# A new order and new engines for the tasks between two phases of an attention and mixture-of-experts kernel

## The chip, the cores and the metric

The kernel runs on one core of a Trainium2 chip. A core has five engines that run side by side, each with its own queue of instructions in a fixed order: TensorE (PE: matrix products and transposes), VectorE (DVE), ScalarE (ACT), GpSimd (POOL, which here also issues the indirect transfers) and SyncE (SP, which issues the other transfers). They wait for one another through semaphores. The metric is the time of one execution in microseconds (us); lower is better. It was measured three times before the change, and once more under the profiler.

## What is computed

Linear attention, and behind it a layer of eight experts in which each token goes to one:

```python
# q, k, v: 8 batches x 8 heads x 576 tokens x 64
q_s = softmax(q, axis=-1);  k_s = softmax(k, axis=2)        # k over the tokens
kv  = einsum('bhsd,bhse->bhde', k_s, v)
x   = einsum('bhsd,bhde->bhse', q_s, kv)  ->  (8, 576, 512)
logits = x @ w_gate                        # 8 experts
gate   = sigmoid(x @ w_local)
for b, s in order:
    e = argmax(logits[b, s]) if s == 0 or gate[b, s] < 0.5 else the expert of token s-1
    out[b, s] = softmax(logits[b, s])[e] * (relu(x[b, s] @ w1[e]) @ w2[e])
```

w1 is 512 x 1024 and w2 1024 x 512 for each expert. There are 4608 tokens.

## The kernel before, in words

**Stages.** For each of the eight batches b a k/v pair is loaded and reduced to one product per head: tasks `Lk, Lv, max, kT, kr, ka, sub, exp` (the exponential of k), `vc` (v copied beside a column of ones), `mul` (the product, PE), `nsum, norm` (divided by its sums), `turn, hi, lo, KW, put` (its product with the gate's weights). "The first product of the seventh pair" is `mul.6.0`. The q side runs over four tiles t of two batches and nine pieces c of 128 x 512: `Lq` loads, `qm` takes the maxima, `qs` subtracts them (line 431), `qT` turns the piece on PE (line 440), `qe` takes the exponential (ACT, line 443), `xm` multiplies with the k/v products into PSUM (line 455), `xc` copies the result to SBUF (line 190 on ACT, 192 on DVE), and after three pieces `inv, xs, ex, gs` take the reciprocals, store the rows to DRAM (888 KB) and form the gate's logits.

**Choosing.** When tiles 0 and 1 are through, `g, Sa, Sb, g1 to g4, ra, rp, rb, ac` (mostly DVE) find each token's expert and its rank, `ro.t.c` (18 of them for these tiles; line 614 on DVE, two instructions of lines 618 and 619 on ACT) write one-hot rows, `ab, am, ax` turn them into the row indices `gidx` (line 678), and `ai, aj` say which expert each block has. `Sc` and the store `Sd.0` give each token's share.

**Blocks.** Tokens are sorted by expert into blocks of 128. The first nine, the early blocks, hold tokens of tiles 0 and 1 alone, so they start while tiles 2 and 3 are still under way. `W.0` to `W.3` load the first expert's weights in quarters of 1 MB (SP). Each weight is cut into a high and a low half-precision part, in 16 pieces: `Wh.i` (line 190) and `Wl.i` (line 955 on DVE; on POOL two instructions), `Wh.12` to `Wh.15` from `W.3`. `G.b` gathers a block's rows (POOL, line 844), `Gp.b` its shares, `Px, Ph, Pl` scale and cut them, and `T.0` (PE) or the transfer `D.b` (SP, line 880) turns them. `F1.b.g` and `F2.b.g` (lines 903, 906 and 926) are the halves of the block's two products, `Ar, Al` the activation in two parts between them, `Gv, Pt` the scaled output and its store. `RN` and `s1, s2` renew the weights where the next block has another expert.

**What sets the order.** All of these tasks are registered with an engine, and some with a second one. A list written out by hand, `ORDER`, gives the order in which they are emitted, and so each engine's queue; the names in `SWAP` go to their second engine. Buffers are rings that are handed round in the order of emission: three for `qs`, three for the copied rows `xt`, two PSUM buffers `pq` shared by `qT`, `turn`, `KW`, `g1`, `rp` and `am`, and for tiles 2 and 3 one, `px`, between `xm` and `xc`. The engine and the registration of the tasks named here:

```python
        eng = alt if name in self.swap else eng                                    # line 65
        add(("Wh", i), ACT, cut_hi, alt=DVE, after=[("W", i // 4)])                # line 1092
        add(("Wl", i), DVE, cut_lo, alt=POOL, after=[("Wh", i)])
```

Of the kernel before, what the change touches and what calls it, by code (L numbers as in the profile page):

```python
# [104 lines left out]


SWAP = """
Ph.0 Ph.11 Ph.2 Ph.3 Ph.4 Ph.6 Ph.9 Pl.6 Pl.8 Px.0 Px.10 Px.4 Px.5 Px.6 Px.9 Wh.15 ex.1.2 ex.3.0 ex.3.2 gs.0.0 gs.0.1 gs.0.2 gs.1.0 gs.1.1
gs.2.0 gs.2.1 gs.2.2 gs.3.0 gs.3.2 norm.3 norm.5 norm.6 put.0 put.2 put.3 put.4 put.6 put.7 qs.2.4 qs.3.6 qs.3.7 ro.0.0 ro.0.2 ro.0.3 ro.0.5 ro.0.7
ro.0.8 ro.1.3 ro.1.7 ro.2.0 ro.2.1 ro.2.2 ro.2.4 ro.2.6 ro.3.0 ro.3.4 ro.3.6 sub.6.1 vc.0.0 vc.0.1 vc.1.0 vc.2.0 vc.3.0 vc.4.0 vc.4.1 vc.5.0 xc.0.0  # L110
xc.0.2 xc.3.5 xc.3.8
"""
# [19 lines left out]
nsum.7 ro.0.0 xm.2.4 ro.0.1 ro.0.4 norm.7 ow ro.0.6 ai turn.6 xc.2.4 hi.6 Lq.3.1 W.0 lo.6 qe.2.6 ro.1.2 xm.2.5 xc.2.5 turn.7 aj.p0 hi.7 lo.7 ex.2.0
ro.1.7 qT.2.7 qe.2.7 qs.2.8 qT.2.8 qe.2.8 ro.1.6 gs.2.0 KW.6 ro.1.5 ro.0.2 xm.2.6 xc.2.6 qs.3.0 qs.3.1 put.6 qT.3.0 xm.2.7 ro.0.5 xc.2.7 ro.0.7 qs.3.2
KW.7 put.7 qe.3.0 xm.2.8 xc.2.8 ab.p0 ro.0.8 qT.3.1 qe.3.1 W.1 inv.2.1 ex.2.1 xs.2.1 qs.3.3 Wh.6 qs.3.4 Wh.3 xm.3.0 xc.3.0 ro.1.0 ab.p1 aj ab ro.1.8
Wh.7 Wh.0 qm.3.1 am ax.p0 ax Wl.3 qT.3.2 qe.3.2 xm.3.1 xc.3.1 qT.3.3 qe.3.3 Wh.1 Sc.0 Wl.7 Wl.0 qT.3.4 Wl.6 qs.3.5 qs.3.6 qs.3.7 G.0 G.1 xm.3.2 xc.3.2
Px.0 Ph.0 Pl.0 qT.3.5 qe.3.5 W.2 qe.3.4 Sd.0 xm.3.3 xc.3.3 qT.3.6 Wh.2 xm.3.4 xc.3.4 Wl.1 W.3 G.2 G.3 Wh.5 Wh.4 qT.3.7 Wl.2 T.0 Tc.0 G.4 Wh.11 Wh.12
Px.1 inv.2.2 xm.3.5 xc.3.5 Wl.4 F1.0.0 Wh.10 Wl.5 qs.3.8 Wh.9 qe.3.6 xs.2.2 qT.3.8 Wl.10 Wl.9 Gp.0 Ph.1 Pl.1 ex.2.2 qe.3.7 xm.3.6 Wh.8
Wl.11 Wl.8 D.1 s1.0 Ar.0.0 Al.0.0 RN.1.0 xc.3.6 F1.0.1 Wl.12 qe.3.8 Wh.13 xm.3.7 Wh.15 Wl.15 Gp.1 Gp.2 xc.3.7 Ar.0.1 F2.0.0 Gp.3 F1.1.0
Al.0.1 RN.1.1 s1.1 Wl.13 Wh.14 gs.2.2 Wl.14 xm.3.8 xc.3.8 Px.2 G.5 G.6 s2.0 Ph.2 Pl.2 Ar.1.0 F2.0.1 RN.1.2 Al.1.0 Gv.0 RN.1.3 gs.2.1
F1.1.1 RN.2.1 Px.3 D.2 RN.2.0 inv.3.1 Px.4 ex.3.1 Ph.3 Pt.0 F2.1.0 Ph.4 Ar.1.1 Pl.3 D.3 Al.1.1 G.7 F1.2.0 Px.5 Ar.2.0  # L140
Al.2.0 s2.1 RN.2.2 Pl.4 D.4 s1.2 RN.3.0 inv.3.2 inv.3.0 gs.3.1 ex.3.2 Ph.5 F2.1.1 Gv.1 F1.2.1 F2.2.0 RN.2.3 ex.3.0 gs.3.0 s2.2 RN.3.2
Ar.2.1 Al.2.1 F1.3.0 RN.3.1 s1.3 F2.2.1 RN.4.0 gs.3.2 g.1.p0 G.8 Px.6 Ph.6 Ar.3.0 Pt.1 oh Gv.2 g.1.p1 g.1 Al.3.0 Pt.2 F1.3.1 g1.1
RN.4.1 F2.3.0 g2.1 g3.1 Ar.3.1 F1.4.0 Al.3.1 g4.1 ra.1 rp.1 Pl.5 RN.3.3 bc.p0 bc.p1 Pl.6 s2.3 D.5 bc D.6 bi.p0 Ar.4.0 Al.4.0
F2.3.1 Gv.3 bi Px.7 Ph.7 Px.8 RN.4.2 Pt.3 RN.4.3 F1.4.1 F2.4.0 rb.1.p0 s1.4 RN.5.0 Ar.4.1 xs.3.0 rb.1 ro.2.8 ro.3.7 RN.5.1 F1.5.0 Gp.4
ro.2.4 ro.2.6 s2.4 RN.5.2 Al.4.1 bb.p0 Pl.7 D.7 F2.4.1 Ar.5.0 Al.5.0 ro.2.5 F1.5.1 Ph.8 Pl.8 bj.p0 s1.5 bj.p1 xs.3.1 bj.p2 RN.6.0 Gv.4
Pt.4 ro.3.0 bj.p3 bj.p4 Ar.5.1 RN.5.3 RN.6.1 Gp.5 Al.5.1 Gp.6 bj ro.2.3 s1.6 F2.5.0 ro.3.8 Gp.7 xs.3.2 F1.6.0 bb bo.2 bo.1
ro.3.4 Ar.6.0 Al.6.0 ro.3.3 F2.5.1 ro.3.5 Sa.1 ro.2.0 Gv.5 RN.7.0 s2.5 RN.6.2 F1.6.1 Ar.6.1 ro.2.2 RN.7.1 RN.6.3 F2.6.0 F1.7.0 bo.3 D.8
Al.6.1 ro.3.6 s2.6 F2.6.1 ro.3.1 s1.7 RN.8.0 ro.2.1 Gv.6 Ar.7.0 RN.7.3 RN.7.2 bo.0 ro.3.2 bm.3 ro.2.7 Al.7.0 bm.1 bm.2 bm.0 bx.p0 bx
Sb.1 F1.7.1 Pt.5 Ar.7.1 Sc.1 Al.7.1 F2.7.0 F1.8.0 F2.7.1 s2.7 G.9 RN.8.2 Px.9 Ph.9 G.10 G.11 Pt.6 RN.8.1 s1.8 RN.8.3 s2.8
Px.10 Pl.9 Ar.8.0 Al.8.0 RN.9.0 Gv.7 Px.11 Ph.10 Pl.10 F1.8.1 T.9 RN.9.1 Tc.9 Sd.1 s1.9.0 s1.9.1 G.12 Ar.8.1 Al.8.1 F2.8.0 T.10 Tc.10 Pt.7 Ph.11 Pl.11  # L150
Gp.8 Gp.9
"""


# [1099 lines left out]
```

## Time and profile before

| | |
|---|---|
| three runs | 545.34, 548.05, 548.52 us (median 548.05) |
| the profiled execution | 545.22 us, of which the span 543.4 us |
| busy over the span | PE 494.1 us (91%), DVE 278.2 (51%), POOL 253.6 (47%), ACT 220.8 (41%) |
| one weight quarter / one store of rows | 1024.0 KB / 888.0 KB |

The page cuts the span into 40 slices of 13.6 us; PE's busy tenths there:

```profile
PE   1668796787999999999999999999999999999995
```

Up to the tenth slice PE has gaps, from the eleventh on it is full to the end. A busy PE is not yet a fast one: its clock is granted at one of two levels (1.2 and 2.4 GHz), and the profile gives it in each stretch as a share of the full one.

### The profile page before, as it was taken

Reading aid. Unit: us, or ns where it says so; the run is one execution under the profiler, and the core shown is the slowest. Engines: PE = TensorE matmul, PEld = TensorE weight load, DVE = VectorE, ACT = ScalarE, POOL = GpSimd, SP = SyncE. Lnnn points to the kernel's source line nnn. Section 1 sums busy time; section 2 is a strip of 40 time slices with the busy share of each in tenths; the row PEclk is TensorE's granted clock in tenths of the full one; section 3 lists DMA queues with packets and bytes.
Section 4 is the critical chain, followed back from the end, with each engine's and each line's share of the span. In section 5 each row is a group of like instructions: output and inputs, shape, how many; then the busy total and the mean of one; then the engine's idle time right before and its main releaser. Section 6 shows DMA issues by size and latency. Waiting matters only on the chain. (4 is left out here: it accounts for less than half of the span.)

```text
span 543.4 us, 19390 instructions
## 1 busy us (share of the span) xinstructions
PE 494.1 (91%) x7314; PEld 367.2 (68%) x7314; DVE 278.2 (51%) x505; ACT 220.8 (41%) x388; POOL 253.6 (47%) x280
## 2 busy tenths in 40 slices
PE   1668796787999999999999999999999999999995
...
GB/s 310 374 382 310 279 331 391 158 336 197 135 82 83 126 112 298 213 244 231 83 83 275 196 75 147 272 130 89 159 295 117 75 73 85 86 84 70 100 76 63
DMA packets 83822, 98.17 MB, mean 181 GB/s; under 512 B 44895, under 2 KB 61279, under 8 KB 83680
## 3 DMA queue, kind: packets, MB, share of 16 engines
...
## 5 line engine op out<-in xcount | busy, mean ns | idle before, releaser
L903 PE MATMUL ph<-xT,w1h 128*128 128x128 f16 (+1 forms) x2432 | 179.9, 217 | 0.4 <-issue 0.4
L903 PEld LDWEIGHTS <-w1h 128*128 128x128 f16 x2432 | 144.3, 98 | 1.3 <-issue 1.3
L933 POOL DMA_INDIRECT out<-y,sidx x38 | 40.0, 1053 | 177.5 <-ACTq L971 150.4
L915 DVE SCALAR_TENSOR_TENSOR lo<-ph,hi 128x512 f16<-128x512 f32 x76 | 52.3, 689 | 133.3 <-ACTq L971 126.5
L911 ACT ACTIVATE hi<-ph 128x512 f16<-128x512 f32 x76 | 45.3, 596 | 176.0 <-PE ph L903 122.8
L906 PE MATMUL ph<-xT,w1l 128*128 128x128 f16 (+1 forms) x1216 | 115.4, 217 | 0.9 <-issue 0.9
L906 PEld LDWEIGHTS <-w1l 128*128 128x128 f16 x1216 | 81.7, 98 | 17.6 <-issue 0.7
L926 PEld LDWEIGHTS <-hi 128*128 128x128 f16 x608 | 56.0, 98 | 54.4
L926 PE MATMUL py<-w2h,hi 128*128 128x512 f16 x184 | 69.8, 379 | 0.0
L926 PE MATMUL py<-w2h,lo 128*128 128x512 f16 x184 | 69.7, 379 | 0.0
L926 PE MATMUL py<-w2l,hi 128*128 128x512 f16 x184 | 69.7, 379 | 0.0
L867 DVE SCALAR_TENSOR_TENSOR x<-xn,x 128x512 f16<-128x512 f32 x39 | 31.7, 812 | 71.5 <-ACT x L190 70.6
L844 POOL DMA_INDIRECT xg<-xrows,gidx x42 | 48.9, 1163 | 23.8 <-DVE tz L679 12.1
L926 PEld LDWEIGHTS <-lo 128*128 128x128 f16 x304 | 29.7, 98 | 35.9
L926 PE MATMUL pi<-w2h,hi 128*128 128x512 f16 x120 | 45.5, 379 | 0.0
L926 PE MATMUL pi<-w2l,hi 128*128 128x512 f16 x120 | 45.5, 379 | 0.0
L926 PE MATMUL pi<-w2h,lo 128*128 128x512 f16 x120 | 45.5, 379 | 0.0
L850 POOL DMA_INDIRECT pb<-shares,gidx x39 | 41.3, 1060 | 8.2 <-issue 7.2
L431 POOL TENSOR_TENSOR qs<-qt,qm 128x512 f32<-128x512 f32 x33 | 34.8, 1065 | 19.0 <-PE pq L440 17.5
L855 POOL TENSOR_TENSOR xn<-xg 128x512 f32<-128x512 f32 x35 | 37.1, 1062 | 9.0 <-DVEq L971 3.2
L322 DVE TENSOR_REDUCE KM<-KT 128x128 f32<-128x1152 f32 x16 | 34.5, 2167 | 4.9 <-DMA KT<-in_k 4.9
L455 PE MATMUL px<-R,qe 64*64 64x74 f32 x864 | 24.5, 256 | 13.2 <-ACT xt L190 6.1
...
## 6 DMA issues: line engine op xcount, KB each, us to landing
...
xrows<-xt SPq DMA_DIRECT2D x12, 888.0 KB
...
s<-in_moe_w SPq DMA_DIRECT2D x4, 1024.0 KB
```

The source lines that it names most:

```text
L322: nc.vector.tensor_reduce(out=KM[b % 2][:, 2 * u:2 * u + 2], in_=KT[b % NKT][:, u:KG:2].rearrange("p g c d -> p g d c"), axis=AX.X, op=ALU ...
L431: on("qs", t, c).tensor_tensor(out=qs[t, c].rearrange("p (g x) d -> p g x d", x=2), in0=qt[t, u][:, :, i, :].rearrange("p (x g) d -> p g x ...
L844: nc.gpsimd.indirect_dma_start(out=xg[b % AHEAD], out_offset=None, in_=src, in_offset=bass.IndirectOffsetOnAxis(ap=i_[:, j_:j_ + 1], axis=0))
L850: nc.gpsimd.indirect_dma_start(out=pb[b % NPB], out_offset=None, in_=src, in_offset=bass.IndirectOffsetOnAxis(ap=i_[:, j_:j_ + 1], axis=0))
L855: eng.tensor_tensor(out=xn[b % 2].rearrange("p (g x d) -> p g x d", g=4, x=2), in0=xg[b % AHEAD].rearrange("p (g x) -> p g x", g=4)[:, :, ...
L867: nc.vector.scalar_tensor_tensor(out=x2[b % 2][:, 1, :], in0=xn[b % 2], scalar=XS, in1=x2[b % 2][:, 0, :], op0=ALU.mult, op1=ALU.subtract)
L903: nc.tensor.matmul(ph_[:, f, 0:n], W["w1h"][:, c, fs], xT_[:, i, c, 0:n], start=False, stop=(c == 3 and i == 1))
L906: nc.tensor.matmul(ph_[:, f, 0:n], W["w1l"][:, c, fs], xT_[:, 0, c, 0:n], start=(c == 0), stop=False)
L911: nc.scalar.activation(hi[b % 2][:, 4 * g:4 * g + 4, :], phs[g], AF.Relu)
L915: nc.vector.scalar_tensor_tensor(out=lo[b % 2][:, gs_, :], in0=phs[g], scalar=0.0, in1=hi[b % 2][:, gs_, :], op0=ALU.max, op1=ALU.subtract)
L926: nc.tensor.matmul(result(b), h_[:, f, :], w_[:, f, :], start=(f == 0 and i == 0), stop=(f == 7 and i == 2))
L933: nc.gpsimd.indirect_dma_start(out=outr, out_offset=bass.IndirectOffsetOnAxis(ap=i_[:, j_:j_ + 1], axis=0), in_=ys[b % 2], in_offset=None, ...
```

## The change

The list `ORDER` is rewritten from behind `mul.6.0` to the middle of the early block 1, and `SWAP` with it; all in front and all behind is as before (the first 321 of 799 names and the last 231 keep their places, the 247 between them are put in another order). Thirty-one tasks change their engine. From POOL to DVE go `qs.2.6, 2.7, 2.8, 3.0, 3.2, 3.3, 3.5, 3.8`, `gs.2.0` to `gs.2.2`, `ex.2.2, ex.3.1, Px.1, Px.2`; from ACT to DVE `norm.6, put.6, put.7, ro.0.0, ro.0.7, ro.1.7`; from DVE to ACT `ro.0.1, ro.1.0, ro.1.2, ro.1.4, ro.1.8, xc.3.5, Wh.15`; from ACT to POOL `vc.7.0, vc.7.1`; from DVE to POOL `Wl.2`. No task is added or removed.

```diff
 SWAP = """
-Ph.0 Ph.11 Ph.2 Ph.3 Ph.4 Ph.6 Ph.9 Pl.6 Pl.8 Px.0 Px.10 Px.4 Px.5 Px.6 Px.9 Wh.15 ex.1.2 ex.3.0 ex.3.2 gs.0.0 ...
+vc.0.0 vc.0.1 put.0 vc.1.0 vc.2.0 put.2 vc.3.0 norm.3 put.3 vc.4.0 vc.4.1 put.4 vc.5.0 norm.5 sub.6.1 vc.7.0 vc.7.1 ...
 ORDER = """
...
-xc.1.8 inv.1.2 exp.7.0 ex.1.1 gs.1.1 put.4 ex.1.2 gs.1.2 exp.6.0 qT.2.1 qe.2.1 xm.2.0 xc.2.0 qT.2.2 qe.2.2 qs.2.3 qT.2.3 mul.6.0 vc.6.1 qe.2.3 ...
+xc.1.8 inv.1.2 exp.7.0 ex.1.1 gs.1.1 put.4 ex.1.2 gs.1.2 exp.6.0 qT.2.1 qe.2.1 xm.2.0 xc.2.0 qT.2.2 qe.2.2 qs.2.3 qT.2.3 mul.6.0 exp.7.1 xs.1.2 ...
...
```

On ACT, from the copies of tile 3 to block 0's activation. `COPY xt` is `xc`, `qe` is `qe`, `w1h` and `w2h` are the cuts `Wh`, `x` is `Ph.1` and `hi` is `Ar.0.0`. Before:

```order
L190 ACTIVATE w1h<-s_1934 128x4x128
L190 COPY xt<-px 128x592
L190 ACTIVATE w1h<-s_1934 128x4x128 x2
L190 ACTIVATE w2h<-s_1935 128x512 x4
L443 ACTIVATE qe<-pq 128x512
L190 ACTIVATE x_1956<-xn_1954 128x512
L443 ACTIVATE qe<-pq 128x512
L190 ACTIVATE w2h<-s_1935 128x512
L911 ACTIVATE hi_1973<-ph_1979 128x512
```

The copy in the second row is `xc.3.4`; behind it come `Wh.5, Wh.4`, then `Wh.11, Wh.12, Wh.10, Wh.9`, of which only `Wh.12` needs the last quarter. Now (lines count two less):

```order
L188 ACTIVATE w2h<-s_2114 128x512
L188 COPY xt<-px 128x592
L188 ACTIVATE w2h<-s_2114 128x512 x4
L441 ACTIVATE qe<-pq 128x512 x2
L188 ACTIVATE w2h<-s_2114 128x512
L188 ACTIVATE x_2135<-xn_2133 128x512
L188 COPY xt<-px 128x592
L909 ACTIVATE hi_2152<-ph_2158 128x512
```

Behind `xc.3.4` (second row) the four cuts `Wh.14, Wh.13, Wh.12, Wh.15`, all of the last quarter, stand in front of `qe.3.6, qe.3.7, Wh.9, Ph.1` and `xc.3.5`; the cuts of the other quarters have moved ahead of `xc.3.4`.

On POOL, from the subtractions `qs` to the first gathers. Before:

```order
L431 TENSOR_TENSOR qs<-qt,qm 128x512 x3
L477 TENSOR_TENSOR ex<-xt 128x216
L431 TENSOR_TENSOR qs<-qt,qm 128x512 x3
L844 DMA xg_1949<-xrows,gidx_72 128x592
L844 DMA xg_1950<-xrows,gidx_72 128x592
L844 DMA xg_1951<-xrows,gidx_72 128x592
L844 DMA xg_1952<-xrows,gidx_72 128x592
L844 DMA xg_1949<-xrows,gidx_72 128x592
L855 TENSOR_TENSOR xn_1954<-xg_1950 128x512
```

Now:

```order
L190 COPY VP_118<-VT_113 128x2x9x64 x2
L475 TENSOR_TENSOR ex<-xt 128x216
L429 TENSOR_TENSOR qs<-qt,qm 128x512
L475 TENSOR_TENSOR ex<-xt 128x216
L429 TENSOR_TENSOR qs<-qt,qm 128x512
L842 DMA xg_2128<-xrows,gidx_72 128x592
L842 DMA xg_2129<-xrows,gidx_72 128x592
L842 DMA xg_2130<-xrows,gidx_72 128x592
L848 DMA pb_2140<-shares,gidx_72 128x1
L842 DMA xg_2131<-xrows,gidx_72 128x592
L949 TENSOR_TENSOR s_2113<-s_2113,wsc 128x4x128
L951 TENSOR_TENSOR w1l<-s_2113,w1h 128x4x128
```

Two subtractions of tile 3 stay in front of the gathers; `vc.7` has come (first row), the first gather of shares `Gp.0` stands in front of `G.3`, and `Wl.2`, the last two rows, behind it.

On the other queues: PE has `xm.3.7` behind `F1.1.1`, and `F1.0.1` directly behind `F1.0.0`. SP has `xs.2.1` behind `W.2` (it was ahead), `s1.0` ahead of `xs.2.2` and `D.1` (it was behind both), and `D.2` ahead of `s2.0`. ACT has `Ar.1.0` behind `Gv.0` (it was ahead). DVE takes `qs.2.6` and the others between the steps of choosing, and the second half of `aj` behind the indices.

## Rows read from the trace of the kernel before

**Rows 1.** windows: stretch, length, busy PE, PEld, DVE, ACT, POOL, PEclk, DMA, GB/s.

```profile
120.00:130.00 10.00, 6.99 (x134) 5.56 (x130) 9.33 (x23) 6.85 (x13) 7.02 (x7) 0.83 0.66 175
130.00:132.00 2.00, 0.39 (x22) 0.39 (x26) 0.40 (x1) 1.09 (x2) 0.02 (x1) 1.00 1.03 393
240.00:300.00 60.00, 60.00 (x719) 43.43 (x717) 28.74 (x42) 26.70 (x47) 26.84 (x24) 1.00 0.62 168
```

**Rows 2.** PE timeline: start, length, engine, line, operation, operands, count.

```profile
135.21 0.61 PE L906 MATMUL ph<-xT,w1l 128*128 128x128 f16 x4
...
142.44 0.75 PE L455 MATMUL px<-R,qe 64*64 64x74 f32 x32
143.12 0.39 PE L926 MATMUL py<-w2h,hi 128*128 128x512 f16 x1
...
145.72 0.39 PE L906 MATMUL ph<-xT,w1l 128*128 128x128 f16 x4
```

**Rows 3.** PE waits from 96 to 150 us: total, times, longest.

```profile
PE px L455 <- ACT xt L190: 6.1, 6, 3.2
```

**Rows 4.** ACT groups, 100 to 135 us: busy, mean ns, idle before, releasers.

```profile
L190 ACT COPY xt<-px 128x592 f32<-128x592 f32 x12 | 7.8, 654 | 5.9 <-PE px L455 3.0 <-issue 2.9
```

**Rows 5.** ACT timeline; in brackets the idle time before it and its releaser.

```profile
104.87 0.43 ACT L618 ACTIVATE da<-iot,off 128x128 f32<-128x128 f16 x1
...
105.86 0.40 ACT L618 ACTIVATE da<-iot,off 128x128 f32<-128x128 f16 x1
...
108.50 0.65 ACT L190 COPY xt<-px 128x592 f32<-128x592 f32 x1 [0.75 <-PE px L455]
...
126.93 1.09 ACT L443 ACTIVATE qe<-pq 128x512 f32<-128x512 f32 x2
130.91 0.65 ACT L190 COPY xt<-px 128x592 f32<-128x592 f32 x1 [2.88 <-issue]
...
132.43 0.65 ACT L190 COPY xt<-px 128x592 f32<-128x592 f32 x1 [0.34 <-PE px L455]
...
135.48 1.67 ACT L190 ACTIVATE w2h<-s 128x512 f16<-128x512 f32 x3 [0.83 <-issue]
```

**Rows 6.** DVE timeline.

```profile
94.91 1.54 DVE L431 TENSOR_TENSOR qs<-qt,qm 128x512 f32<-128x512 f32 x1
...
106.05 0.54 DVE L614 TENSOR_SCALAR oo<-iot,off,val 128x128 f16<-128x128 f16 x2
...
121.50 1.05 DVE L678 TENSOR_SCALAR gidx<-tk 128x9 int32<-128x9 f32 x1
122.47 0.16 DVE L679 TENSOR_SCALAR tz<-tk 128x9 f32<-128x9 f32 x1
...
126.57 1.33 DVE L431 TENSOR_TENSOR qs<-qt,qm 128x512 f32<-128x512 f32 x2
...
136.38 1.44 DVE L955 SCALAR_TENSOR_TENSOR w1l<-s,w1h 128x512 f16<-128x512 f32 x2
```

**Rows 7.** POOL timeline.

```profile
121.46 1.06 POOL L431 TENSOR_TENSOR qs<-qt,qm 128x512 f32<-128x512 f32 x1 [1.43 <-PE pq L440]
122.85 1.70 POOL L844 DMA_INDIRECT xg<-xrows,gidx  x1 [0.33 <-DVE tz L679]
124.85 1.42 POOL L844 DMA_INDIRECT xg<-xrows,gidx  x1 [0.30 <-issue]
...
175.08 1.56 POOL L864 TENSOR_SCALAR xn<-xn 128x512 f32<-128x512 f32 x1
176.72 1.16 POOL L865 TENSOR_TENSOR x<-xn,x 128x512 f16<-128x512 f32 x1
```

**Rows 8.** SP timeline: transfers issued.

```profile
125.44 0.37 SPq L965 DMA_DIRECT2D s<-in_moe_w  x1
135.39 0.34 SPq L466 DMA_DIRECT2D xrows<-xt  x1
139.65 1.37 SPq L880 DMA_TRANSPOSE xT<-x  x1
```

More of the change, by code (lines that the diff above doesn't have):

```diff
@@ L107 @@
 SWAP = """
[L108 to L111, printed above, removed]
+vc.0.0 vc.0.1 put.0 vc.1.0 vc.2.0 put.2 vc.3.0 norm.3 put.3 vc.4.0 vc.4.1 put.4 vc.5.0 norm.5 sub.6.1 vc.7.0 vc.7.1 xc.0.0 xc.0.2 gs.0.0 gs.0.1 gs.0.2
+gs.1.0 gs.1.1 ex.1.2 qs.2.4 qs.2.6 qs.2.7 qs.2.8 ex.2.2 qs.3.0 qs.3.2 ex.3.0 gs.3.0 qs.3.3 qs.3.5 ex.3.1 qs.3.6 qs.3.7 qs.3.8 xc.3.8 ex.3.2 gs.3.2
+ro.0.1 ro.0.2 ro.0.3 ro.0.5 ro.0.8 ro.1.0 ro.1.2 ro.1.3 ro.1.4 ro.1.8 ro.2.0 ro.2.1 ro.2.2 ro.2.4 ro.2.6 ro.3.0 ro.3.4 ro.3.6 Wl.2 Px.0 Ph.0 Px.1 Px.2
+Ph.2 Ph.3 Px.4 Ph.4 Px.5 Px.6 Ph.6 Pl.6 Pl.8 Px.9 Ph.9 Px.10 Ph.11
 """
@@ L128 @@
 xc.1.5 inv.1.1 qs.2.0 qT.1.7 qT.1.8 qe.1.7 qe.1.8 xm.1.6 qm.2.1 xc.1.6 xm.1.7 xc.1.7 qs.2.1 qT.2.0 qe.2.0 xm.1.8 KW.5 vc.6.0 xs.1.1 KW.4 qs.2.2 put.5
-xc.1.8 inv.1.2 exp.7.0 ex.1.1 gs.1.1 put.4 ex.1.2 gs.1.2 exp.6.0 qT.2.1 qe.2.1 xm.2.0 xc.2.0 qT.2.2 qe.2.2 qs.2.3 qT.2.3 mul.6.0 vc.6.1 qe.2.3 g.0.p0
-g.0.p1 g.0 g1.0 Sa.0 Sb.0 xm.2.1 xs.1.2 exp.6.1 qs.2.4 qT.2.4 qe.2.4 xc.2.1 g2.0 vc.7.0 vc.7.1 qm.3.0 g3.0 g4.0 ra.0 xm.2.2 mul.6.1 xc.2.2 nsum.6 rp.0
-rb.0.p0 qs.2.5 qT.2.5 norm.6 exp.7.1 xm.2.3 xc.2.3 qs.2.6 qs.2.7 inv.2.0 rb.0 qe.2.5 ro.1.3 ro.0.3 ac mul.7.0 mul.7.1 xs.2.0 ro.1.1 qT.2.6 ro.1.4
@@ L132 @@
[L132 to L151, printed above, removed]
+xc.1.8 inv.1.2 exp.7.0 ex.1.1 gs.1.1 put.4 ex.1.2 gs.1.2 exp.6.0 qT.2.1 qe.2.1 xm.2.0 xc.2.0 qT.2.2 qe.2.2 qs.2.3 qT.2.3 mul.6.0 exp.7.1 xs.1.2 g.0.p0
@@ new lines @@
+g.0.p1 qs.2.4 g.0 qm.3.0 exp.6.1 qe.2.3 g1.0 xm.2.1 vc.6.1 xc.2.1 g2.0 qT.2.4 qs.2.6 g3.0 g4.0 qs.2.5 xm.2.2 qe.2.4 xc.2.2 ra.0 qT.2.5 rp.0 xm.2.3
+qe.2.5 Sa.0 qs.2.7 rb.0.p0 xc.2.3 rb.0 mul.6.1 ro.1.2 ro.1.7 nsum.6 qT.2.6 xm.2.4 vc.7.0 inv.2.0 ro.0.3 norm.6 ro.1.1 mul.7.0 ac ro.1.8 qe.2.6 Sb.0
+vc.7.1 qs.2.8 ro.0.5 ab.p0 ro.0.7 xc.2.4 mul.7.1 turn.6 qT.2.7 hi.6 xm.2.5 ro.1.3 xc.2.5 xm.2.6 xs.2.0 ab.p1 ab ro.0.1 lo.6 qe.2.7 qT.2.8 ro.1.6
+ro.1.5 qe.2.8 xc.2.6 nsum.7 qs.3.2 norm.7 ai KW.6 ro.1.4 turn.7 xm.2.7 hi.7 inv.2.1 put.6 aj.p0 Lq.3.1 qs.3.0 ro.0.0 qT.3.0 ro.0.2 qs.3.3 xc.2.7
```

16 lines of the change are left out of this document (added).

## The prediction

> **What bounds the kernel now.** I read the stretch windows first. From 240 to 300 us TensorE (PE) is busy 60.00 of 60 us at the full clock, while from 120 to 130 us it is busy 6.99 of 10 [rows 1]. So the kernel has two parts: a front in which PE starves, and the blocks, in which PE sets the pace. A change to the front is worth what it shifts the moment at which PE stops starving, and no more. Next the PE timeline [rows 2]: block 0's first product F1.0.0 starts at 135.21, its second product F2.0.0 at 143.12, and F1.1.0 of block 1 at 145.72. The yardstick of this prediction is the start of F1.1.0. In the new order xm.3.7 (0.68 us, the step from 142.44 to 143.12 [rows 2]) is left until after it, so breaking even means F1.1.0 at 145.72 - 0.68 = 145.04.
>
> What holds the front? The waits view names ACT's copies xc: PE waits for them 6.1 us in six waits, 3.2 at once [rows 3]. For tiles 2 and 3 there is one px buffer, so xm and xc alternate strictly. ACT's groups show the other side [rows 4]: from 100 to 135 us ACT is idle 5.9 us in front of these copies, 3.0 of them for PE and 2.9 at one place, before 130.91 [rows 5], whose end the profile does not explain. Between copies the ACT timeline [rows 5] shows the exps qe, the permutation rows ro and the weight cuts Wh. VectorE (DVE) is fuller still: 9.33 of 10 us from 120 to 130 [rows 1].
>
> **The change, part by part.**
>
> *Step 1, DVE up to the row indices.* Ahead of gidx (121.50) the change puts six more subtractions qs on DVE, 6 x 0.67 = +4.0 (two end to end take 1.33 [rows 6]), and one cut Wl.0, +0.7 (two take 1.44 [rows 6]). Three permutation rows come and five go, 2 x 0.27 = -0.5 (two take 0.54 [rows 6]); norm.6 and two puts come and the second half of aj goes, which I set at nothing, with bounds of -0.5 and +0.5. That is +4.2 of work. Against it stands a gain that the order does not show: a DVE instruction that overlaps a POOL subtraction (1.06 us at 121.46 [rows 7]) is stretched. A subtraction on DVE takes 1.54 beside one and 0.67 otherwise, and gidx, beside the one at 121.46, takes 1.05 where its like takes 0.16 [rows 6]. So each costs DVE up to 0.87 to 0.89; I take 0.8. Of ten POOL subtractions in this stretch three stay; of the seven that go, I count one as costing nothing: 6 x 0.8 = -4.8. Net -0.6: gidx, and with it the gather G.0 (122.85 [rows 7]), come about when they did. The bounds are +4.2 (nothing given back) and -1.1 (0.89 each).
>
> The Trainium skill (SBUF — State Buffer, section "SBUF: two separate sides") says that DVE and GpSimd share a port pair by an exclusive lock, held for a whole instruction. By that rule a removed POOL subtraction can return all of its 1.06 us: 6.4 in place of 4.8, and DVE 1.6 earlier; the stretched rows agree in kind and lie below it in size. The same rule speaks against one move, the cut Wl.2 sent to POOL, which could block DVE for as long as that cut's two instructions run.
>
> *Step 2, ACT and the px rounds.* From xc.2.4 (108.50) to xc.3.4 (132.43 [rows 5]) ACT gets five more cuts Wh, 5 x 0.56 = +2.8 (three take 1.67), and one ro more, +1.0 (from one at 104.87 to the next at 105.86), and loses one qe, -0.55 (two take 1.09 [rows 5]), and two small puts, which I leave out: +3.2 in all. The cover is the 5.9 us of idle time [rows 4]. If the 2.9 us return and only 3.0 can be filled, xc.3.4 comes at 132.43 + 0.2 = 132.6; if all of it fills, at 132.43 - 5.9 + 3.2 = 129.7. I take 129.7, since the order gives that wait no cause and ACT now has cuts ready at hand. F1.0.0 followed xc.3.4 by 135.21 - 132.43 = 2.8 (transposes and xm.3.5, which stay in front of it), so F1.0.0 comes at 132.5, at the latest at 135.4. From there PE needs 10.51 to F1.1.0 as before, less 0.68: 142.3 if nothing else holds it.
>
> *Step 3, the cuts of the last weight quarter.* W.3 is issued at 125.44 [rows 8], right behind the shares' store Sd.0, and ACT's first cut from it starts at 135.48 after 0.83 us of idle [rows 5]. In the new order all four such cuts stand in front of qe.3.6, qe.3.7, Wh.9, Ph.1 and xc.3.5 in ACT's queue. Call ACT's start on them L. Wh.9 ends at L + 2.2 (four cuts) + 1.1 (two qe) + 0.55 = L + 3.85; then come DVE's Wl.9, qs.3.8, Px.2, Wl.15 and Pl.1, 5 x 0.67 = 3.35: L + 7.2 for the transpose D.1, issued at 139.65 before. From issue to first use it has had between 1.37 (its issue alone [rows 8]) and 6.07 (to 145.72); I take 3.7, the middle. So F1.1.0 cannot start before L + 10.9. L is bounded below by the issue plus one megabyte at the 393 GB/s of 130 to 132 us, 125.4 + 2.7 = 128.1 [rows 1, 8], and above by today's 135.48, since W.3's issue stays near where it was: a qs and all of aj (together 1.4) now stand in front of Sc.0, and gidx's stretch of 0.9 and step 1's 0.6 are gone. The nearest row is today's own; two gathers, G.3 and G.4, of 128 x 592 x 4 bytes = 0.3 MB each, now come behind it, 0.6/0.393 = 1.5 us less traffic. L = 134.0 puts F1.1.0 at 144.9, against 145.04: **-0.1 us**.
>
> *What is moved besides, set at nothing.* On SP, xs.2.1 goes behind W.2: 1 MB, 2.7 us later; only xc.3.3 (130.91 [rows 5]) needs its buffer. s1.0 goes ahead of xs.2.2 and D.1; it waits for Wl.6, some 5 us before D.1 can go, and xs.2.2 went out only at 135.39 anyway [rows 8]. Without that cover D.1 would queue behind a store of 0.9 MB, 2.3 us. On ACT, Ar.1.0 goes behind Gv.0, which waits for F2.0.1; then Gv.0, Ar.1.0 and DVE's Al.1.0 take some 3 x 0.7, while PE has xm.3.7 and F1.1.1, as many columns as the 2.6 us of F2.0.0 (143.12 to 145.72 [rows 2]). vc.7 moves to POOL, which then has nothing else to do ahead of mul.7.
>
> **Sum.** The profiled execution took 545.22 us, its span 543.4; with -0.1 it is 545.1. It is the lowest of the four executions shown (545.34, 548.52 and 548.05 are the others); their mean is 546.8, the median of the three 548.05, 2.8 above the profiled one. I put the new median near that mean: 546.8 - 0.1 = 546.7, and say **546.5 us**, since the bounds on L reach further down than up.
>
> **The rivals.**
> *A, the full gain* (0.20). ACT starts on W.3 by 131.4, so that L + 10.9 stays under 142.3 and step 2's chain decides. For it: DMA moves only 175 GB/s from 120 to 130 us [rows 1]. Against: today's ten microseconds from issue to cut. Then -2.7; with the first rounds, too, a few microseconds earlier up to -6: 544 to 541.
> *B, POOL late with Wl.2* (0.18, the other side). POOL's queue is now G.0, G.1, G.2, Gp.0, G.3, Wl.2, and Gp.0 waits for Sd.0. A cut on POOL is two instructions; the nearest rows are 1.56 and 1.16, and 1.42 for each of Gp.0 and G.3 [rows 7]. It decides from the point where Sd.0 lands later than 132.5 - 2.72 - 2.84 = 126.9. If Sd.0 takes the 10.04 us that W.3's first cut took, Wl.2 ends at 125 + 10 + 5.5 = 140.5, F1.0.0 or its later columns lose 5 to 8 us, F1.1.0 comes at 147.3 to 150.3: +2.3 to +5.3, 549 to 552.
> *C, DVE gets nothing back* (0.15). Step 1 at +4.2 in place of -0.6 pushes Sc.0, W.3 and L by up to 4.8: +1.5 to +4.7, 548 to 551.5. Against it: the stretched rows.
> *D, the unexplained 2.9 us return* (inside the forecast): F1.0.0 at 135.4, F1.1.0 at 145.2, +0.2.
>
> **How the numbers follow.** Forecast 0.47: L between 131.4 and 135.5 gives -2.7 to +1.4. A 0.20, B 0.18, C 0.15. One per cent, about what a measurement of this kernel can tell from no change, is 5.5 us. Only the far ends of A, B and C reach it; I add the spread of the executions, 3.2 us from lowest to highest, and leave more than half of A, and of B and C together, inside. Faster 0.13, within 1% 0.74, slower 0.13. The range reaches from A's lower end, 541.5, to B's upper end, 552.
>
> **What would show it.** Step 1: DVE's qs at about 0.67 each and G.0 within 1.5 us of 122.85. Step 2: hardly any ACT idle time between xc.2.4 and xc.3.4, and F1.0.0 near 132.5. Step 3: ACT idle in front of the cut Wh.14, PE gaps in front of qT.3.8, F2.0.0 or F1.1.0, and F1.1.0 near 144.9. The prediction is wrong if F1.0.0 is held inside with POOL named (B), or if PE runs without a gap from F1.0.0 on (A).

## The result and the profile after

The changed kernel is slower: ratio 1.0085 [1.0056, 1.0113], on 21 executions of each. The median of before was 547.73 us, so that is +4.7 us, 552.4, where 546.5 was forecast (541.5 to 552.0). The executions of after spread more than those of before (547.7 to 559.6 against 545.3 to 552.1); the ratio leaves out the seven that lie more than 1.5% above its fastest, and the median of all 21 is 554.5. The profiled one is among these seven: 559.6, with a span of 557.9. So I read each stretch against a second profile of the same kernel, from a chip on which before takes 543.5 (the first experiment: 550.9, span 549.1), and use what both show. In the kernel's body the line numbers of after are 2 lower.

The first loss lies in mul.7, the product of the eighth and last k/v pair. Its waits stand in the groups of TensorE from 90 to 115 us of before and from 90 to 118 of after (line, operation, operands, count | busy us, mean ns | idle before and releaser):

```profile
L373 PE MATMUL pk<-VP,KT 64*64 64x65 f32 x288 | 5.4, 224 | 1.5 <-issue 1.5
```
```profile
L371 PE MATMUL pk<-VP,KT 64*64 64x65 f32 x288 | 6.2, 248 | 4.9 <-issue 4.2 <-DVE R L392 0.7
```

The same engine and line in time (start, length; in brackets the idle time before), before first, then after, then after's second profile:

```profile
102.98 2.31 PE L373 MATMUL pk<-VP,KT 64*64 64x65 f32 x139
106.83 0.34 PE L373 MATMUL pk<-VP,KT 64*64 64x65 f32 x5 [1.54 <-issue]
```
```profile
104.15 0.75 PE L453 MATMUL px<-R,qe 64*64 64x74 f32 x32
105.61 1.75 PE L371 MATMUL pk<-VP,KT 64*64 64x65 f32 x104 [0.71 <-DVE R L392]
111.54 1.36 PE L371 MATMUL pk<-VP,KT 64*64 64x65 f32 x40 [4.17 <-issue]
...
114.30 1.27 PE L453 MATMUL px<-R,qe 64*64 64x74 f32 x32
```
```profile
105.77 1.75 PE L371 MATMUL pk<-VP,KT 64*64 64x65 f32 x104 [0.49 <-DVE R L392]
111.69 1.36 PE L371 MATMUL pk<-VP,KT 64*64 64x65 f32 x40 [4.17 <-issue]
```

PE stops inside one product, and no semaphore that the profile shows ends the wait: "issue". Before it stops after 139 of 144 pairs of instructions, for 1.54 us; after the change after 104 pairs, for 4.17. The new order puts qT.2.6 (4 pairs) and xm.2.4 (32) in front of mul.7, and 139 - 36 is 103: the stop is, within a pair, at the same place of PE's program. It moves with the count of instructions and not with the work, which points at the loading of the program. The page of after has a DMA queue for that (packets, MB, share of 16 engines):

```profile
q8 instruction: 82, 1.34, 1.0%
```

1.34 MB in 82 packets are 16 KB each. In the DMA view of after, the stretches 104.3 to 109.2 us (first row) and 109.2 to 110.3 (the two others) show:

```profile
q1 hardware_dynamic: 249, 1.02, 65.3%
...
q1 hardware_dynamic: 400, 0.40, 102.9%
q8 instruction: 1, 0.02, 5.5%
```

For 4.9 us no code moves; then one packet does, at the start of the second stretch, and PE goes on 2.3 us behind it. Up to 105.96 the queues are empty, and why the code isn't sent then is open. What fills them from there is xs.2.0, the store of 888 KB of token rows, which SP issues at 105.14 (`xrows<-xt`, before at 103.60); its packets run from 105.96 to 108.72, and the code follows at 109.26, among the first packets of the load that SP issued next. In before the code's packet is sent between 104.4 and 104.6, among the first of that store, and PE goes on 2.3 us later as well; the stretch 103.2 to 105.5 of before:

```profile
q1 hardware_dynamic: 61, 0.43, 46.5%
q8 instruction: 1, 0.02, 2.6%
```

The idle time is not all. The windows of after behind it (columns as in [rows 1]):

```profile
107.00:111.50 4.50, 0.36 (x26) 0.22 (x15) 2.49 (x12) 1.93 (x5) 0.00 (x0) 0.93 1.02 318
111.50:118.00 6.50, 5.69 (x112) 4.87 (x113) 3.18 (x15) 3.10 (x7) 0.56 (x1) 0.50 0.05 16
118.00:124.00 6.00, 5.68 (x88) 4.22 (x87) 4.89 (x12) 5.18 (x13) 1.58 (x2) 0.50 0.89 310
```

PE was idle from 107.4 to 111.5, and then the granted clock is 0.50, its lower level of 1.2 GHz, for 12.5 us; a px product takes 1.27 us instead of 0.75. In before, behind the idle 1.54, 107 to 113 shows 0.64. The second profile of after has 0.50 up to 124 as well. Not all of that is the stop's doing: a third profile of after, without a stop (part 4 below), has such a stretch later:

```profile
116.50:126.70 10.20, 8.23 (x140) 6.69 (x141) 9.08 (x27) 8.52 (x18) 5.21 (x6) 0.50 1.04 379
```

From the end of mul.6.0 to F2.1.0 the second profile takes 4.6 us more than the third; PE is idle 2.6 us more in it and busy 2.0 us more, at a mean granted clock of 0.86 in place of 0.88.

The rows of the forecast's yardsticks in after: gidx and G.0, F1.0.0, F2.0.0, F1.1.0, then xm.3.7 and the second product of block 1 (for [rows 2, 6, 7]):

```profile
126.95 0.17 DVE L676 TENSOR_SCALAR gidx<-tk 128x9 int32<-128x9 f32 x1
...
128.03 1.67 POOL L842 DMA_INDIRECT xg<-xrows,gidx  x1 [2.26 <-DVE w1l L953]
...
139.39 0.40 PE L904 MATMUL ph<-xT,w1l 128*128 128x128 f16 x4
...
146.42 0.39 PE L924 MATMUL py<-w2h,hi 128*128 128x512 f16 x1
...
150.31 0.38 PE L904 MATMUL ph<-xT,w1l 128*128 128x128 f16 x4 [0.25 <-DMA xT<-x]
...
159.14 0.84 PE L453 MATMUL px<-R,qe 64*64 64x74 f32 x23
160.39 0.35 PE L453 MATMUL px<-R,qe 64*64 64x74 f32 x3 [0.40 <-issue]
161.10 0.38 PE L453 MATMUL px<-R,qe 64*64 64x74 f32 x6 [0.36 <-issue]
161.85 0.44 PE L924 MATMUL py<-w2h,hi 128*128 128x512 f16 x1 [0.37 <-issue]
```

F1.1.0 is at 150.31; 145.04 was break-even and 144.9 the forecast. The first part of the front, which is unchanged, differs by up to 3.3 us between profiles, so I count from the end of mul.6.0, the last task that both orders share (L, as in the prediction, is ACT's start on the cuts of W.3):

| profile | stop in mul.7 | gidx | L | F1.0.0 | F1.1.0 | F2.1.0 |
|---|---|---|---|---|---|---|
| before | 1.54 | 25.5 | 39.5 | 39.2 | 49.8 | 58.5 |
| before, again (below) | 2.05 | 27.1 | 40.4 | 37.2 | 51.5 | 60.2 |
| after | 4.17 | 29.2 | 42.3 | 41.7 | 52.6 | 64.1 |
| after, second | 4.17 | 29.5 | 43.2 | 43.2 | 53.5 | 63.0 |
| after, third (below) | none | 25.1 | 38.6 | 38.8 | 48.9 | 58.4 |
| inv.2.0 later (below) | 0.61 | 25.6 | 39.7 | 37.7 | 50.0 | 59.5 |

From F2.1.0 on, before takes 388.9 us to its end, the second and third profile of after 388.7 and 387.7. So the time is lost ahead of F2.1.0: 4.5 us in after's second profile and 5.6 in its first, of which 2 are the torn xm.3.7 (2.71 us from its start to the next product, before 0.68). Before's own two profiles differ by 1.7 us there. (The first profile of after loses another 7.1 us behind F2.1.0, 4.4 of them between 226 and 250, which the second doesn't repeat.)

### The profile page after: what moved, and what is told of

It reads as the page before. It is cut to its first block, busy times and chain, and to the rows that moved or that the text cites. A ratio compares the mean times of both kernels' runs of the same rounds, so it can differ in the third digit from the quotient of the medians.

```text
span 557.9 us, 19370 instructions
## 1 busy us (share of the span) xinstructions
PE 504.0 (90%) x7314; PEld 373.0 (67%) x7314; DVE 278.2 (50%) x518; ACT 220.8 (40%) x386; POOL 240.8 (43%) x263
## 3 DMA queue, kind: packets, MB, share of 16 engines
q8 instruction: 82, 1.34, 1.0%
## 5 line engine op out<-in xcount | busy, mean ns | idle before, releaser
L931 POOL DMA_INDIRECT out<-y,sidx x38 | 40.1, 1056 | 191.8 <-ACTq L969 152.6
L842 POOL DMA_INDIRECT xg<-xrows,gidx x42 | 47.0, 1119 | 26.2 <-DVE tz L677 11.9
L848 POOL DMA_INDIRECT pb<-shares,gidx x39 | 40.8, 1047 | 10.3 <-issue 7.5
L853 POOL TENSOR_TENSOR xn<-xg 128x512 f32<-128x512 f32 x33 | 34.9, 1059 | 8.7 <-DVE x L865 4.9
L453 PE MATMUL px<-R,qe 64*64 64x74 f32 x864 | 26.5, 262 | 9.6 <-issue 3.9
L371 PE MATMUL pk<-VP,KT 64*64 64x65 f32 x1152 | 26.5, 248 | 9.0 <-issue 8.1
```

What stands on the lines that cost most here:

```text
L371: nc.tensor.matmul(pks[b][64 * x:64 * x + 64, i, (D + 1) * m:(D + 1) * (m + 1)], KT[b % NKT][ps, g, c], VP[b % 2][ps, g, c], start=(c == 0 ...
L842: nc.gpsimd.indirect_dma_start(out=xg[b % AHEAD], out_offset=None, in_=src, in_offset=bass.IndirectOffsetOnAxis(ap=i_[:, j_:j_ + 1], axis=0))
L848: nc.gpsimd.indirect_dma_start(out=pb[b % NPB], out_offset=None, in_=src, in_offset=bass.IndirectOffsetOnAxis(ap=i_[:, j_:j_ + 1], axis=0))
L853: eng.tensor_tensor(out=xn[b % 2].rearrange("p (g x d) -> p g x d", g=4, x=2), in0=xg[b % AHEAD].rearrange("p (g x) -> p g x", g=4)[:, :, ...
L931: nc.gpsimd.indirect_dma_start(out=outr, out_offset=bass.IndirectOffsetOnAxis(ap=i_[:, j_:j_ + 1], axis=0), in_=ys[b % 2], in_offset=None, ...
```

## The experiments

The letters in the expectations are those of theories on the result, not of the prediction's rivals; A is that PE's code comes late inside mul.7, because the store's packets are in front of it. Ratios are against before on the same chip.

**1. Is the stop the cause?** xs.2.0 needs the reciprocals inv.2.0 on VectorE; moved behind ac, it lets the store go a little later, while PE's program stays. Two halves of the order alone, and the changed kernel again, ran beside it.

```diff
 e2_inv_later (after)
-... xm.2.4 vc.7.0 inv.2.0 ro.0.3 norm.6 ro.1.1 mul.7.0 ac ro.1.8 ...
+... xm.2.4 vc.7.0 ro.0.3 norm.6 ro.1.1 mul.7.0 ac inv.2.0 ro.1.8 ...
 e3_new_then_old: after's order through xs.2.0, before's behind it
-... xc.2.5 xm.2.6 xs.2.0 ab.p1 ab ro.0.1 lo.6 qe.2.7 ...
+... xc.2.5 xm.2.6 xs.2.0 ro.1.4 nsum.7 ro.0.0 ro.0.1 ...
 e4_old_then_new: before's through xs.2.0, after's behind it
```

> The changed kernel once more, for a second profile. Theory A (late code): TensorE runs dry in the last k/v product because its next 16 KB block of instructions (DMA queue 8) is fetched behind the rows transfer that SP issues 0.85 us after TensorE enters its last loaded block; this belongs to the order, so the idle time put down to issue before that product (4.17 us in the first profile, 1.54 us before the change) is above 3 us again, and F1.0.0 starts at 138 to 140. Theory B (accident of one execution): it is under 2 us, F1.0.0 starts at 135.5 to 137, and the time is nevertheless about 554 us, so the loss lies elsewhere.

> The changed order with the one task inv.2.0 (two short VectorE instructions that release the rows transfer) moved behind the task ac, so that SP issues that transfer 1.5 to 2 us later. Theory A: the fetch goes ahead of the transfer, the idle time in the last k/v product falls from 4.17 to under 1.5 us, and the time falls from 554 to 549 to 551 us. Theory B: idle time and time stay as in the changed kernel (553 to 556 us).

> The changed order and engines up to the issue of the rows transfer xs.2.0, the order and engines of before from there on. Theory A: the long wait for code is in this first part, so the ratio to before is 1.005 to 1.010 (550.5 to 553 us). Theory C (the loss is in the second part, with xm.3.7 behind F1.1.1 and the new order of the weights): ratio 0.998 to 1.003.

> The order and engines of before up to xs.2.0, the changed ones from there on. Theory A: idle time before the rest of the last k/v product about 1.5 us as before, ratio to before 0.998 to 1.003. Theory C: 1.006 to 1.012.

Measured: after again 1.0112 [1.0083, 1.0142], stop 4.17 again; **inv.2.0 later 1.0036 [1.001, 1.0062]**, stop 0.61:

```profile
103.76 1.75 PE L371 MATMUL pk<-VP,KT 64*64 64x65 f32 x104 [0.48 <-DVE R L392]
106.12 0.81 PE L371 MATMUL pk<-VP,KT 64*64 64x65 f32 x40 [0.61 <-issue]
```
```profile
106.10:112.00 5.90, 4.52 (x128) 3.49 (x128) 5.70 (x30) 5.68 (x13) 0.51 (x1) 0.96 0.96 316
```

Same place, 3.6 us less idle time, and the clock stays at 0.96 in the window behind it. The medians are 549.42 and 545.57: 3.85 of the 5.95 us that the change costs on this chip go with one small move on VectorE. Counted from the end of mul.6.0 the store is issued 10.2 us behind in place of 7.4 and 7.9, its packets run from 106.0 on, and the code's packet leaves between 103.4 and 103.6, into an empty queue; PE goes on 2.6 us behind that. The first half alone is 1.0144 [1.011, 1.0178], the second alone 1.0061 [1.0036, 1.0085]: the loss sits mostly in the first half, but the second has a share of its own, against A's expectation, and the two don't add up to the whole. The profile of the first half fell on its one execution at 545.88 (the others took 549.95 to 552.34): there mul.7 runs in one piece of 144, without a stop. So the stop looks like a race that some executions win; the slower ones have no profile.

**2. Move the boundary, not the work.** Tiny products on scratch columns at the start shift PE's program and nothing else; before again is the control. The other way round, before with inv.2.0 early issues its store sooner.

```diff
 e5_after_shift16 (after), e8_before_shift42 (before), e17_after_shift8 (after): 16, 42 and 8 products
+        for _ in range(16 if b == 0 else 0):
+            nc.tensor.matmul(kxs[b][0:64, 0:1], ident[0:64, 0:64], ident[0:64, 0:1], start=True, stop=True)
 e11_before_inv_early (before)
-... rp.0 rb.0.p0 qs.2.5 qT.2.5 norm.6 exp.7.1 xm.2.3 xc.2.3 qs.2.6 qs.2.7 inv.2.0 rb.0 ...
+... rp.0 inv.2.0 rb.0.p0 qs.2.5 qT.2.5 norm.6 exp.7.1 xm.2.3 xc.2.3 qs.2.6 qs.2.7 rb.0 ...
```

> The changed kernel, order untouched, with 16 tiny extra products at the very start of TensorE's queue, where it is idle for 7 us (their output is overwritten). They put every later block of instructions 64 of TensorE's instructions earlier in the stream. Theory A (late code): TensorE passes into its last loaded block about 1 us earlier (103.3 in place of 104.3 us), the fetch goes ahead of the rows transfer, the 4.17 us of idle time in the last k/v product fall to under 1 us, and the time falls from 549.4 to 544 to 546.5 us. Theory F (the stall belongs to the work itself: semaphores, operands, weights): idle time and time stay (4 us, 549 us). The other blocks' ends move too, so the time may shift by a further us either way; the idle time decides.

> The kernel before once more, as a control and for a second profile of it: ratio 0.997 to 1.003; idle time put down to issue in the last k/v product 1 to 2 us (1.54 in the first profile); F1.0.0 to F2.1.0 19.2 us as in the first profile.

> The kernel before, order untouched, with 42 tiny extra products at the very start of TensorE's queue: the block ends move by 168 instructions, so that TensorE passes into its last loaded block just after SP issues the rows transfer (about 103.9 us) and not 0.4 us ahead of it. Theory A: the 1.5 us of idle time inside the last k/v product go, and a wait put down to issue of 2 to 3.5 us appears 35 to 45 pairs of products later (between 106.5 and 111 us); time 543.5 to 547 us. Theory F: idle time stays inside the last k/v product at 1.5 us, nothing new behind it.

> The kernel before with inv.2.0 moved ahead of rb.0 (four short VectorE instructions earlier), so that SP issues the rows transfer about 1 us earlier, 0.6 us ahead of TensorE's step into its last loaded block and not 0.4 us behind it. Theory A: the fetch is caught behind the transfer, the idle time in the last k/v product grows from 1.5 to 2.1 us (two profiles) to 3 to 4.5 us, ratio 1.003 to 1.009. Theory F: idle time 1.5 to 2.1 us, ratio 0.998 to 1.002.

> The changed kernel with 8 tiny extra products at the start of TensorE's queue (idle there; output overwritten): blocks of instructions end 32 instructions earlier, and TensorE enters the last loaded block about 0.7 us earlier against the issue of the rows transfer. Theory A (race for the code): no execution is caught, idle time inside mul.7 under 1.2 us, the upper group of times goes, ratio 0.998 to 1.003 (the changed kernel 1.005, 1.0085 and 1.011). If the two groups come from elsewhere: ratio 1.004 to 1.011.

That the boundary moves with the count is best seen in e18 of part 4, the mended kernel with 8 products (16 pairs) in front. After 104 - 16 = 88 pairs it stops:

```profile
105.47 1.52 PE L373 MATMUL pk<-VP,KT 64*64 64x65 f32 x88
107.28 1.05 PE L373 MATMUL pk<-VP,KT 64*64 64x65 f32 x56 [0.29 <-issue]
```

In the three shifted kernels here mul.7 ran in one piece of 144. The times don't follow as cleanly: 16 products 1.0058 [1.0026, 1.0089], with a new wait for issue of 1.53 us at 115.95 and a front that ran some 3 us late; 8 products 1.003 [0.9994, 1.0066], and its profiled execution, without a stop, is at 547.15 one of the five slower of its twelve (547.2 to 548.3; the others 542.9 to 545.5), so slower executions remain that this stop doesn't explain; 42 products ahead of before 1.006 [1.0027, 1.0092], where they alone took 9.1 us at the start and the expected new stop did not come, so that one tells nothing. The control was 1.0005 [0.9974, 1.0037], with a stop of 2.05: before has one in any case.

Before with inv.2.0 early got the stop that was expected, at before's own place:

```profile
104.19 2.31 PE L371 MATMUL pk<-VP,KT 64*64 64x65 f32 x139
110.03 0.34 PE L371 MATMUL pk<-VP,KT 64*64 64x65 f32 x5 [3.52 <-issue]
...
133.57 0.75 PE L453 MATMUL px<-R,qe 64*64 64x74 f32 x32 [2.77 <-ACT xt L188]
```

Its DMA view from 104.4 to 107.6 us has the store and no code:

```profile
q1 hardware_dynamic: 237, 1.01, 98.9%
```

So a store moved earlier lengthens the stop, in the old order too: 1.54 became 3.52. The code's packet leaves between 107.6 and 107.8, 2.3 us ahead of PE. But the time is 1.0016 [0.9989, 1.0044], below the 1.003 to 1.009 expected. Of the 2 us, gidx is late by 1.6 against before's profile (27.1 behind mul.6.0), F1.0.0 only by 0.9 (40.1): part of it may go into a wait for ACT that before's order has in any case (2.77 here at 133.57; [rows 3] has 3.2). After's longest wait of PE for these copies is 1.7 us, so it has less to take a delay up with; that this is why it pays in full is argued, not shown. F2.1.0 is late by 2.6 (61.1), but 1.8 of that is a px product at 140.72 that is torn as after's xm.3.7 is.

**3. Mend the tail.** With the stop small, PE still has waits of 3.4 us between 129 and 145 us. In the kernel with inv.2.0 later:

```profile
130.56 0.56 PE L872 MATMUL pt<-id,x 128*128 128x128 f16 x7 [0.97 <-DVE x L865]
...
132.71 0.38 PE L904 MATMUL ph<-xT,w1l 128*128 128x128 f16 x4
...
135.13 0.40 PE L904 MATMUL ph<-xT,w1l 128*128 128x128 f16 x4 [0.92 <-POOL w1l L951]
...
139.85 0.63 PE L438 MATMUL pq<-ident,qs 128*128 128x128 f32 x4 [0.52 <-DVE qs L429]
...
142.41 0.39 PE L924 MATMUL py<-w2h,lo 128*128 128x512 f16 x1 [0.71 <-DVEq L969]
...
145.00 0.38 PE L904 MATMUL ph<-xT,w1l 128*128 128x128 f16 x4 [0.26 <-DMA xT<-x]
```

F1.0.0 is held inside for Wl.2, as the prediction's rival B has it, and POOL's rows show why (Gp.0 waits for the shares, the cut comes behind it):

```profile
129.72 1.00 POOL L848 DMA_INDIRECT pb<-shares,gidx  x1 [3.36 <-DMA shares<-pr]
131.02 1.41 POOL L842 DMA_INDIRECT xg<-xrows,gidx  x1 [0.30 <-issue]
132.45 1.05 POOL L949 TENSOR_TENSOR s<-s,wsc 128x512 f32<-128x512 f32 x1
133.58 1.49 POOL L951 TENSOR_TENSOR w1l<-s,w1h 128x512 f16<-128x512 f32 x1
```

```diff
 e7_mended (e2, and): Wl.2 on DVE behind Tc.0; Pl.0, qs.3.8, Pl.1 and Al.0.0 earlier on DVE
-... T.0 Tc.0 G.2 qT.3.7 ... G.3 Wl.8 Wl.2 ... xm.3.5 Wl.9 F1.0.0 F1.0.1 qs.3.8 xc.3.5 Px.2 s1.0 Ar.0.0 ...
+... T.0 Tc.0 Wl.2 G.2 qT.3.7 ... G.3 Wl.8 ... xm.3.5 qs.3.8 Wl.9 F1.0.0 F1.0.1 xc.3.5 Pl.1 s1.0 Ar.0.0 Al.0.0 Px.2 ...
 e9_mended2 (e7, and): Wh.0 behind xc.2.8, Wl.0 behind ax
 e10_wl2_dve (e2, and): Wl.2 on DVE behind Tc.0, nothing else
 e12_mend_only (after, and): e7's moves without that of inv.2.0
 e15_mended2_x37 (e9, and): F1.1.1 behind xm.3.7
```

> The changed order with inv.2.0 behind ac as in e2, and the four waits that TensorE has between 129 and 145 us in e2 taken away: Wl.2 back on VectorE behind Tc.0, Pl.0 ahead of qs.3.7, qs.3.8 ahead of Wl.9, Pl.1 and Al.0.0 ahead of Px.2 and Wl.15. Theory D (these waits are what is left of the loss): TensorE's idle time from 129 to 145 us falls from 3.4 to about 1 us, F2.1.0 starts 1.5 to 2.5 us earlier than in e2 (154.5), time 543 to 544.5 us. Rival (the landing of the last weights of the first block sets F1.1.0 whatever VectorE does): F2.1.0 within 0.7 us of e2's, time 545 to 546 us.

> e7 with two more moves: Wh.0 behind xc.2.8 on ScalarE and Wl.0 behind ax on VectorE. In e7 TensorE waits 3.00 us ahead of am (at 122.12 us), and ScalarE stands there 1.43 us in Wh.0 for the landing of the first weights, with qe.3.2 and xc.2.8 queued behind it. If that wait is on the path (theory E): idle time ahead of am under 1 us, gidx about 2.5 us earlier, the stretch from the first product of mul.7 to F2.1.0 falls from 48.9 to 46.5 to 48 us, time 541 to 542.5 us (ratio 0.992 to 0.996). Rival: the landing of W.3 sets F1.1.0 and does not move, 48.5 to 49.5 us, ratio as e7 (0.995 to 0.999).

> e2 with Wl.2 alone back on VectorE, behind Tc.0. Rival B of the prediction (Wl.2 on GpSimd, behind Gp.0 and Sd.0, holds F1.0.0): the wait of 0.92 us inside F1.0.0 goes, mul.7 to F2.1.0 falls from 50.8 to 49.5 to 50.3 us, ratio 1.001 to 1.003. If qs.3.8 and the landing of x for F1.1.0 bound what follows: the 0.92 us return as a longer wait ahead of qT.3.8 or F1.1.0 and the ratio stays 1.003 to 1.005.

> The changed order with e7's five moves behind the routing but inv.2.0 left where the change has it. If the late code and the waits of the first block are two separate losses: idle time in the last k/v product about 4.2 us as in the changed kernel, ratio 1.002 to 1.007 (the changed kernel 1.011 less the 0.7% between e2 and e7). If one covers the other: ratio within 0.002 of the changed kernel's or of e7's 0.997.

> e9 with xm.3.7 ahead of F1.1.1 in place of behind it, away from the chain out, xg, pb, xg that GpSimd issues before F2.1.0. Theory G: on a chip with late completions xm.3.7 takes 0.75 us in one piece (2.1 us longer in e9, e10, e12) and the ratio is 1.000 to 1.005 (e9 1.008); on a chip without, 0.992 to 0.997. Rival (xm.3.7 is torn by its own place in the code, whose block ends inside it): the stutter goes on any chip, and none was there in e1, e2 and e7 to go.

Mended (e7): 0.9968 [0.9937, 0.9999], the best of all, with a stop of 1.98; e15, on the chip of part 4: 0.9992 [0.9967, 1.0017]. The three others shared one chip and came out at 1.0082 [1.0052, 1.0111] (e9), 1.0118 [1.0075, 1.0162] (e10) and 1.0086 [1.005, 1.0122] (e12), with stops of 0.34, 0.15 and 0.61. Their single waits moved as meant (e9 has no wait for the exp in front of am, which cost e7 3.00 us; e10 none inside F1.0.0). But e12 shows a stop of 0.61 where 4.2 was expected, and is not faster for it; e10, which has the move of inv.2.0 too, loses as much as after does elsewhere; and all three tear xm.3.7 as after's first profile does (e9: from 155.07 to 157.97, in pieces of 23, 3, 5 and 1).

On this chip and on the result's, something else costs time as well (the last section); verdicts from them alone, on the tail and on the stop's share of the loss, stay open.

**4. Once more, on a fourth chip.** After a third time, mended twice more (the second with 8 products in front), and before with two VectorE tasks put between the gathers, which was to test a theory G of the unexplained waits.

```diff
 e16_before_spread (before)
-... W.3 G.2 G.3 Wh.5 ... Wh.12 Px.1 inv.2.2 ... Wl.5 qs.3.8 Wh.9 ...
+... W.3 G.2 Px.1 G.3 qs.3.8 Wh.5 ... Wh.12 inv.2.2 ... Wl.5 Wh.9 ...
```

> The changed kernel a third time, to have it on the same chip as the next three. Theory A (late code is the larger part wherever it runs): ratio to before 1.007 to 1.013, idle time before the last 40 pairs of mul.7 above 3 us.

> e7's kernel again, beside the changed kernel on one chip. If e7's gain belongs to the order: at least 0.8% below e13 and 0.995 to 1.002 of before, whatever the chip. If the chip decided (theory G: where TensorE's completions come late during chains of gathers, xm.3.7 in its new place costs 2 to 4 us): on a chip whose profiles show late completions 1.003 to 1.009, on one without 0.995 to 0.999.

> The kernel before with its chain of gathers G.0 to G.4 broken up: Px.1 between G.2 and G.3, qs.3.8 between G.3 and G.4. Theory G, on a chip with late completions: the completion that comes 3.0 us late in the first profile of before (ScalarE idle for 2.88 us to 130.91) is at most 1.5 us late, and F1.0.0 starts 1 to 2 us earlier after mul.7; the time changes by -1.5 to +0.5 us. On a chip without late completions: none is late in either, time within 1 us of before.

> e7's kernel with the same 8 extra products. In its three profiles so far the idle time inside mul.7 was 0.9 to 2.0 us; theory A: under 1 us, ratio 0.994 to 0.999, below that of e17 by 0.3 to 0.6%. Rival (the weights' landing covers it): the same ratio as e7 and e14 (0.997 to 1.001).

After took 1.005 [1.002, 1.008] here, and its profile, against the expectation, has no stop:

```profile
106.93 2.28 PE L371 MATMUL pk<-VP,KT 64*64 64x65 f32 x144
```

The code's packet leaves between 106.0 and 106.9, into an empty queue (the DMA view of that stretch); the store is issued 9.2 us behind mul.6.0, not 7.4 and 7.9, and its packets begin at 107.2:

```profile
q8 instruction: 1, 0.02, 6.7%
```

F2.1.0 then comes 58.4 us behind mul.6.0, where before's two profiles have 58.5 and 60.2: about even, as forecast. Mended 1.0005 [0.9986, 1.0024] and, shifted, 0.9998 [0.9967, 1.0029]: even with before, not faster, so e7's lead is not confirmed, and below after by 0.45%, not the 0.8% expected. Before with its tasks spread was 1.0008 [0.9984, 1.0033]; the waits it was made for did not occur on this chip, so it tells nothing.

## Why the prediction was wrong

The step that failed is one that the prediction did not have. Its sum starts at xc.2.4 and lets PE's program ahead of it stand; of that stretch it says only that vc.7 on POOL is free "ahead of mul.7", under what is set at nothing. Yet before's trace had a wait of 1.54 us inside mul.7 without a cause. A wait "issue" in the middle of a product should have been a term with bounds: nothing if it went, and at the upper end the store that follows it, 888 KB or 2.3 us by the prediction's own price for such a store, more with the lower clock behind it. The new order put 36 more pairs in front of mul.7, so that PE needs its next block of code earlier in mul.7, and in after's first two profiles that block left only behind the store. It cost 2.6 us more of idle time than before's stop, and 2.0 us of busy time at the lower clock (second profile against third); one move that takes the long stop away brings back 3.85 of 5.95 us on one chip. What part it has in the 4.7 us of the result's own chip is not shown: the one profile there is 7 us above the ratio's time.

In the prediction's own terms the delay broke the bound on L, "above by today's 135.48, since W.3's issue stays near where it was". W.3 was issued at 131.24 (125.44 before), L came at 140.03 in the first profile and at 140.61 in the second, and F1.1.0 followed:

```profile
131.24 0.37 SPq L963 DMA_DIRECT2D s<-in_moe_w  x1
140.03 2.19 ACT L188 ACTIVATE w2h<-s 128x512 f16<-128x512 f32 x4 [2.20 <-DMA s<-in_moe_w]
```

*Step 1* was right in kind: gidx, no longer beside a POOL subtraction, took 0.17 us for 1.05, and where mul.7 stops little or not at all gidx comes 25.1 to 25.6 us behind mul.6.0, against 25.5: even, forecast -0.6. Rival C (nothing given back, +1.5 to +4.7) fell with that.

*Step 2* was too hopeful: F1.0.0 was to come 2.7 us earlier (132.5 for 135.21). Counted from mul.6.0 it came 1.5 us earlier with inv.2.0 later and 0.4 in after's third profile; that the first of these stands at 132.71 is luck, as its front ran 0.9 us ahead. With the stop it came at 139.39 and 140.60. ACT's idle time in front of the copies fell from 5.9 [rows 4] to 3.3 us (after, 100 to 140 us), not to hardly any.

*Step 3* held in its mechanism: F1.1.0 was to come no earlier than L + 10.9, and it came at L + 10.3 in all three profiles of after and with inv.2.0 later (134.70 and 145.00); in the mended kernel, with three of DVE's tasks moved, 135.90 and 145.01 (L + 9.1). Rival A, the full gain, fell: in after's third profile and with inv.2.0 later L stayed within 0.9 us of before's, counted from mul.6.0.

*Rival B* named a wait that was there, at the wrong size: 0.92 us with inv.2.0 later, and none in after's three profiles, where 5 to 8 in F1.0.0 were priced. From Sd.0's issue to Gp.0 it was 4.3 us in after and 5.4 with inv.2.0 later, where W.3's 10.04 had been taken.

*Rival D*'s 2.9 us at 130.91 did not return in after's three profiles; waits like it came back on the chip of e9 to e12, in either order, as below.

Open: what decides how soon the code is asked for (in e7 its packet left at 106.6 to 106.8, with no store in the way, and mul.7 still stopped for 1.98 us); what the 0.3 to 0.5% are that remain on the fourth chip in profiles of after without a stop; why the halves don't add up; and why e9, e10 and e12 lose as much with a small stop.
